# Takeout and square patterns set chunk by chunk in a DFT and squared-ReLU kernel, with a rearranged head and moved folds, on one Trainium2 core

## The chip, the cores and the metric

The kernel runs on one core of one Trainium2 chip. The metric is device time in microseconds (us), measured over several executions of one launch; the profile gives a span of one execution, which is about 2 us shorter here. Engines are named as in the profile: PE is TensorE (matmul), PEld its weight loads, ACT is ScalarE, DVE is VectorE, POOL is GpSimd, SP is SyncE. A run on one core has no second die to be held against, so a run counts as slow here only when it lies more than 1.5% above the fastest of its kernel.

## The reference

```python
def _attn_ref(x):                       # x: (8, 3008, 256)
    X = np.fft.fft(x, axis=1)
    X = np.fft.fft(X, axis=2)
    return X.real.astype(np.float32)

def _moe_ref(x, w_in, w_out):           # x: (24064, 256), w_in: (256, 2048), w_out: (2048, 256)
    h = np.maximum(x @ w_in, 0.0)
    return (h * h @ w_out).astype(np.float32)

def reference(x, moe_w_in, moe_w_out):
    return _moe_ref(_attn_ref(x).reshape(8 * 3008, 256), moe_w_in, moe_w_out)
```

## The kernel before

The kernel folds each batch of `x` by its symmetries (VectorE adds, "fold"), multiplies it by cosine and sine tables (the "DFT", also called stage 1), and folds the feature DFT into the first weight matrix (`G1`, `G2`, `G3`). Outputs come in mirrored pairs: sequence rows k and 3008 - k share the products with `G1` and `G2`. There are 8 x 1505 = 12040 pairs. They are cut into 25 chunks: chunks 0 and 1 of 256 pairs (8 steps each), chunks 2 to 23 of 512 pairs (16 steps each), chunk 24 of 264 pairs. So steps 0 to 15 are chunks 0 and 1, steps 16 to 31 chunk 2, steps 32 to 47 chunk 3, steps 48 to 63 chunk 4. A letter in `KINDS` says how a step makes the two sides of its pairs:

```python
    KINDS = ["rrrrrrrrrrrrrrrr"] * 3 + ["rrrrrrrrdrrrrrrr"] * 3 + ["rrrrrrdrrrdrqrdr"] + ["rrdrqrdrrrdrqrdr"] * 8 + ["rrrrrrrdqrqdrqdr"] + ["qdqrdqrdqrqdrqdr"] * 8 + ["rrdrdrrdrrdrdrrd"]
    SQA = [()] * 6 + [(2, 6)] * 9 + [(1, 4, 6)] * 9 + [()]    # which pairs of steps ScalarE squares
```

A plain step, `r`, takes three matmuls of 512 columns and two ScalarE relus. A takeout, `d` or `q`, takes two matmuls: before the second one, VectorE (`d`), or ScalarE followed by GpSimd (`q`), copies the first product out, and VectorE later makes the mirrored side from that copy.

```python
    def x_front(c, u):                    # r: G1 and G2 products, relu
        # ... matmuls with G1 (start) and G2 into xb ...
        act(r_s(c, u), xb, AF.Relu, scale=-1.0)                              # L606
        return (c, u, xb, None)

    def x_take(c, u):                     # d or q: G1 product alone, taken out to T
        # ... matmul with G1 into xb ...
        X = edge(c, u)                                                       # L633, VectorE
        if KINDS[c][u] == "q":
            act(T, xb, AF.Copy, bias=0.0, scale=-2.0)                        # L649
            nc.gpsimd.tensor_tensor(T, T, X, op=ALU.add)                     # L650
        else:
            stt(out=T, in0=xb, scalar=-2.0, in1=X, op0=ALU.mult, op1=ALU.add)  # L652
        return (c, u, xb.unsqueeze(1), T)

    def x_back(cur):                      # two steps (LAG) later
        if T is not None:
            # ... matmul with G2 into xb ...
            act(r_s(c, u), xb, AF.Relu, scale=-1.0)                          # L662
            # a step later, VectorE: max(xb + T, 0) reversed into the mirrored side, L663
            return
        # ... matmul with G3 into xb ...
        relu_d(c, u, lambda o, i: act(o, xb[:, :, i], AF.Relu, scale=-1.0))  # L670

    def x_square(cur):                    # every second step, over two steps' h
        if u // 2 in SQA[c]:
            # ... two ScalarE squares of half the tile, L679 and L680 ...
            return
        vt(h2, h2, h2, op=ALU.mult)                                          # L682, VectorE
```

`xb` is one of six PSUM tiles, which the DFT also uses. A chunk's output matmuls (`po`) start when its last square has been issued. The program fixes the order of each engine's instructions. The fold of a batch needs that batch of `x`, 3 MB, whose load is issued inside the fold of the batch before, since there is only one buffer `x4`:

```python
    def fold_ops(b):
        # pair, pair0: adds of x rows and mirrored rows from x4 into u        L333, L337
        ops = [f for s in range(2) for f in (pair(s, 0), pair(s, 1), pair0(s))]
        if b + 1 < B:
            ops.append(lambda: load_x(b + 1))     # POOL issues the DMAs once the adds are done
        # ... half, edges, feat: 14 more VectorE operations, L345 to L361 ...
```

`spread` deals operations evenly over a range of steps, and `FOLD` says over which part of a batch's steps a fold is dealt (batch 1 is steps 32 to 79):

```python
    spread(rd1[2:], 1, 8)                 # reduction for the second sine table
    spread(fo, 7, 12)                     # second half of batch 0's fold
    spread(tr1[0:5], 5, 8)                # Sin and Cos of the second table (ScalarE)
    spread(tr1[5:], 8, 9)
    spread(mi1, 9, 12)
    spread(stage1_ops(0, 1, True), 11, 15)   # second DFT of batch 0
    FOLD = {0: [(1, 0.5, 0.66)], 1: [(2, 0.02, 0.28), (3, 0.3, 0.56), (4, 0.58, 0.85)],
            2: [(5, 0.06, 0.96)], 3: [(6, 0.04, 0.96)], 4: [(7, 0.04, 0.85)]}
    ST1 = {0: (0.66, 0.98)}
    # ... in the loop over steps:
        if len(made) > SQ:                # SQ = 3: squares are issued three steps after the relus
            retire()
```

## Time and profile before

| | before |
|---|---|
| time, median of 4 runs | 615.67 us (615.24 to 615.78) |
| span of the profiled run | 613.2 us |
| matmuls, streamed columns | 4631; 1,380,424 |

The page's first part gives busy time, share of the span and instructions of each engine; its fourth part gives the chain of work that ended last, by engine:

```profile
PE 592.0 (97%) x4631; PEld 443.1 (72%) x4631; DVE 493.4 (80%) x855; ACT 522.9 (85%) x949; POOL 146.6 (24%) x138
...
PE 94%; ACT 2%; DMA 2%; DVE 1%; issue 0%; POOL 0%; DVEq 0%; POOLq 0%; ACTq 0%
```

PE bounds the kernel, but 97% does not say how tightly. The Trainium skill, "Perfetto Trace Analysis", Tensor Engine Instruction, says that the end of a matmul is estimated from its size, and "Trainium Kernel Development and Optimization", Performance Expectations, calls matmul busy time a bad metric. The trace agrees: 512-column matmuls are shown 379 ns long, yet start every 216 ns. So PE time is counted here by starts: in PE's instructions in order of time, the spacing of two starts less the columns of the first times 0.4236 ns is called *extra*. Packed matmuls have next to none. Summed up over the trace of before:

| stretch | us |
|---|---|
| until the first matmul starts | 11.0 |
| streaming of all columns but the last matmul's | 584.6 |
| extra, 0 to 20 us | 3.1 |
| extra, 20 to 45 us | 6.7 |
| extra, 45 us to the end | 3.4 |
| last matmul's start to the end | 4.3 |

There are two ways to shorten it: fewer columns, or the 6.7 us of the head. Here PE in order of time in the head (start, us, engine, line, operation, tiles, count, and in brackets the idle time before it and what ended it):

```profile
31.76 0.38 PE L73 MATMUL xb<-qt,G 128*128 128x256 f16 x2 [0.88 <-ACT h L606]
...
33.40 0.38 PE L73 MATMUL xb<-qt,G 128*128 128x256 f16 x2 [0.83 <-ACT h L606]
...
34.72 0.38 PE L73 MATMUL xb<-qt,G 128*128 128x256 f16 x2 [0.50 <-ACT h L606]
...
36.91 0.38 PE L73 MATMUL xb<-qt,G 128*128 128x256 f16 x2 [1.38 <-ACT h L606]
```

In this stretch PE stands before the third product of each step until ScalarE has done the relu. The first output matmul starts at 40.26 us, so PE has nothing else to do.

### The profile page before, as it was taken

What the parts mean: (1) busy time and instruction counts of PE and PEld (TensorE: products, weight loads), DVE (VectorE), ACT (ScalarE), POOL (GpSimd) and SP (SyncE); (2) the same over time, 40 slices, a digit from 0 to 9 for tenths busy, and PEclk for the clock granted to TensorE, in tenths of its full rate; (3) what the DMA queues carried; (4) which work ended last, traced back from release to release, by engine and by line L of the source; (5) the groups of instructions that cost most, each with busy time, mean ns of one, the idle gap of its engine ahead of it and who ended that gap; (6) DMA issues with size and microseconds to landing.
All of it is one profiled execution on the core that took longest, in us unless ns stands there. A gap on an engine that the chain in (4) does not pass through costs nothing.

```text
span 613.2 us, 12145 instructions
## 1 busy us (share of the span) xinstructions
PE 592.0 (97%) x4631; PEld 443.1 (72%) x4631; DVE 493.4 (80%) x855; ACT 522.9 (85%) x949; POOL 146.6 (24%) x138
## 2 busy tenths in 40 slices
PE   2879999999999999999999999999999999999997
PEld 1556677777777777777777778877787778877786
DVE  8789788976578868886888675799998999999870
ACT  5787888777888898888988888999999999999971
POOL 8303023300050002400101010433333334333200
PEclk9999999999999999999999999999999999999999
DMA  8947498673293134832232213332232322332212
GB/s 267 256 91 196 74 237 218 126 190 68 40 247 57 52 43 70 230 61 41 55 60 41 41 51 46 62 42 55 44 58 56 43 56 58 44 60 54 57 52 71
DMA packets 41824, 56.25 MB, mean 92 GB/s; under 512 B 8158, under 2 KB 37138, under 8 KB 41766
## 3 DMA queue, kind: packets, MB, share of 16 engines
q1 hardware_dynamic: 33878, 29.05, 25.2%
q0 software_dynamic: 7840, 26.40, 17.2%
q8 instruction: 36, 0.59, 0.4%
q14 instruction: 22, 0.18, 0.1%
q10 hardware_dynamic: 48, 0.02, 0.0%
HBM read 29.02 MB, written 24.64 MB: 88 GB/s over the span
## 4 chain that ended last, share of the span: by engine, by line
PE 94%; ACT 2%; DMA 2%; DVE 1%; issue 0%; POOL 0%; DVEq 0%; POOLq 0%; ACTq 0%
PE po L73 54%; PE xb L73 34%; PE pf L73 6%; DMA x<-in_x_dram,idx 2%; ACT h L606 1%; DVE u L333 1%; ACT h L670 1%; ACT cosT L260 0%; ACT G L309 0%; ACT G L308 0%; ACT sinT L264 0%; DVE h L682 0%; DVE v L345 0%; DVE tm L236 0%; DVE qt L426 0%
## 5 line engine op out<-in xcount | busy, mean ns | idle before, releaser
L73 PE MATMUL po<-wout,h 128*128 128x256 f16 x3024 | 450.1, 272 | 0.0
L73 PEld LDWEIGHTS <-h 128*128 128x128 f16 x3024 | 286.0, 98 | 112.2
L73 PE MATMUL xb<-qt,G 128*128 128x512 f16 (+16 forms) x824 | 230.9, 321 | 4.5 <-ACT h L606 3.7
L682 DVE TENSOR_TENSOR h<-h 128x2048 f16<-128x2048 f16 (+1 forms) x147 | 176.0, 1201 | 4.6 <-ACT h L670 4.6
L650 POOL TENSOR_TENSOR bs<-bs,h 128x512 f32<-128x512 f32 x68 | 93.5, 1375 | 345.1 <-ACT bs L649 299.8
L606 ACT ACTIVATE h<-xb 128x512 f16<-128x512 f32 (+1 forms) x229 | 139.0, 607 | 28.4 <-PE xb L73 27.7
L670 ACT ACTIVATE h<-xb 128x512 f16<-128x512 f32 (+1 forms) x239 | 139.9, 592 | 26.3 <-PE xb L73 22.1
L73 PEld LDWEIGHTS <-G 128*128 128x128 f16 x1336 | 127.2, 98 | 30.2 <-issue 5.9
L73 PE MATMUL xb<-pt,G 128*128 128x512 f16 (+16 forms) x512 | 146.4, 323 | 0.1
L663 DVE CUSTOM_DVE_ANT_0 h<-xb,bs 128x512 f16<-128x512 f32 (+2 forms) x161 | 104.7, 654 | 43.5 <-ACT h L662 43.5
L662 ACT ACTIVATE h<-xb 128x512 f16<-128x512 f32 (+1 forms) x155 | 96.0, 620 | 8.0 <-PE xb L73 6.5
L652 DVE SCALAR_TENSOR_TENSOR bs<-xb,h 128x512 f32<-128x512 f32 (+1 forms) x87 | 58.2, 669 | 21.0 <-PE xb L73 17.9
L633 DVE TENSOR_SCALAR h<-eb,gE 128x512 f16<-128x512 f16 (+1 forms) x155 | 66.6, 431 | 0.5 <-DMA eb<-qt 0.5
L557 ACT ACTIVATE os<-po 128x512 f32<-128x512 f32 x94 | 58.0, 617 | 9.4 <-PE po L73 8.9
L680 ACT ACTIVATE h<-h 128x1024 f16<-128x1024 f16 x45 | 48.7, 1082 | 0.0
L679 ACT ACTIVATE h<-h 128x1024 f16<-128x1024 f16 x45 | 47.8, 1063 | 0.0
L649 ACT ACTIVATE bs<-xb 128x512 f32<-128x512 f32 x68 | 42.8, 630 | 0.5
L333 DVE TENSOR_TENSOR u<-x 127x765 f16<-127x765 f32 x32 | 29.7, 948 | 1.8 <-DMA x<-in_x_dram 1.6
L101 POOL DMA_INDIRECT x<-in_x_dram,idx x18 | 26.9, 1492 | 5.5 <-issue 4.8
L124 POOL DMA_DIRECT2D x<-in_x_dram x14 | 8.2, 589 | 76.2 <-DVE u L337 75.3
L73 PEld LDWEIGHTS <-w 127*128 127x128 f16 (+1 forms) x192 | 21.6, 118 | 5.7 <-issue 0.7
L351 DVE TENSOR_TENSOR w<-v 127x381 f16<-127x381 f16 x64 | 21.9, 368 | 0.0
(103 smaller groups left out, 217.9 us busy)
## 6 DMA issues: line engine op xcount, KB each, us to landing
out_dram<-os SPq DMA_DIRECT2D x157, 128.0 KB
x<-in_x_dram POOLq DMA_DIRECT2D x14, 756.0 KB, 11.2
wst<-in_moe_w_in_dram POOLq DMA_DIRECT2D x4, 512.0 KB, 7.3
eb<-qt SPq DMA_DIRECT2D x14, 128.0 KB
x<-in_x_dram SPq DMA_DIRECT2D x2, 756.0 KB
wout<-in_moe_w_out_dram POOLq DMA_DIRECT2D x4, 256.0 KB, 10.3
x<-in_x_dram,idx POOLq DMA_INDIRECT x18, 12.4
gE<-G SPq DMA_DIRECT2D x16, 0.2 KB
```

The costliest lines, as they stand in the source:

```text
L73: nc.tensor.matmul(o, l, r, start=start, stop=stop, skip_group_check=True)
L557: act(os_, po, AF.Copy, bias=0.0, scale=HS * HS)
L606: act(r_s(c, u), xb, AF.Relu, scale=-1.0)
L633: ts(out=X, in0=ebc[c][:, 0:n], scalar1=gE2[:, u : u + 1], scalar2=None, op0=ALU.mult)
L650: nc.gpsimd.tensor_tensor(T, T, X, op=ALU.add)
L652: stt(out=T, in0=xb, scalar=-2.0, in1=X, op0=ALU.mult, op1=ALU.add)
L662: act(r_s(c, u), xb, AF.Relu, scale=-1.0)
L663: mirrors.append((DLAG[KINDS[c][u]], lambda: relu_d(c, u, lambda o, i: nc.vector._custom_dve(TENSOR_ADD_SAT, out=o[:, 0, :], in0=xb[:, 0, ...
L670: relu_d(c, u, lambda o, i: act(o, xb[:, :, i], AF.Relu, scale=-1.0))
L679: act(h2[:, 0:nf], h2[:, 0:nf], AF.Square)
L680: rest.append(lambda: act(h2[:, nf:], h2[:, nf:], AF.Square))
L682: vt(h2, h2, h2, op=ALU.mult)
```

## The change

The intent is to take columns off PE where ACT and DVE had room, and to fill PE's holes in the head. Takeouts go from 155 to 200 and ScalarE squares from 45 to 63, each chunk with a pattern of its own. A new kind `v` is a plain step whose mirrored relu is done by VectorE. Operations of the head and folds of batches 1 to 4 move.

```diff
-    KINDS = ["rrrrrrrrrrrrrrrr"] * 3 + ["rrrrrrrrdrrrrrrr"] * 3 + ["rrrrrrdrrrdrqrdr"] + ["rrdrqrdrrrdrqrdr"] * 8 + ["rrrrrrrdqrqdrqdr"] + ["qdqrdqrdqrqdrqdr"] * 8 + ["rrdrdrrdrrdrdrrd"]
-    SQA = [()] * 6 + [(2, 6)] * 9 + [(1, 4, 6)] * 9 + [()]
+    KINDS = ["vrvrrrrrrrrrrrrr"] + ["rrrrrrrrrrrrrrrr"] + ["rvvrrvrrrrrrrrrr"] + ["rrrrrrrrrrrdrrqr"] + ["rdqqrrqrdrrrqrrq"] + ["rrrqrrrrqrqrdddq"] + # ... chunks 6 to 18 ...
+            ["qqdrddrdrqqdrqdq"] + # ... chunks 20 to 24 ...
+    SQA = [()] + [(3,)] + [(2,)] + [(0, 4, 5)] + [(0, 2, 5, 6)] + # ... + [(1, 4, 5, 6, 7)] for chunk 19 ...
...
+        if KINDS[c][u] == "v":
+            relu_d(c, u, lambda o, i: ts(out=o, in0=xb[:, :, i], scalar1=-1.0, scalar2=0.0,
+                                         op0=ALU.mult, op1=ALU.max))
+            return
...
-    spread(rd1[2:], 1, 8)
-    spread(fo, 7, 12)
-    spread(tr1[0:5], 5, 8)
-    spread(tr1[5:], 8, 9)
-    spread(mi1, 9, 12)
-    spread(stage1_ops(0, 1, True), 11, 15)
-    FOLD = {0: [(1, 0.5, 0.66)], 1: [(2, 0.02, 0.28), (3, 0.3, 0.56), (4, 0.58, 0.85)],
+    spread(rd1[2:], 0, 5)
+    spread(fo, 8, 12)
+    spread(tr1[0:5], 8, 11)
+    spread(tr1[5:], 11, 12)
+    spread(mi1, 11, 12)
+    spread(stage1_ops(0, 1, True), 14, 15)
+    FOLD = {0: [(1, 0.504, 0.773)], 1: [(2, 0.02, 0.256), (3, 0.232, 0.697), (4, 0.562, 0.876)],
...
-    ST1 = {0: (0.66, 0.98)}
+    ST1 = {0: (0.845, 0.944)}
...
-        if len(made) > SQ:
+        while len(made) > (1 if made and made[0][0] < 2 else SQ):
             retire()
```

(A new rule for when the edge rows of a chunk are spread is there to make the new patterns legal.)

More of the change, by code (lines that the diff above doesn't have):

```diff
@@ L487 @@
         g += n
-    KINDS = ["rrrrrrrrrrrrrrrr"] * 3 + ["rrrrrrrrdrrrrrrr"] * 3 + ["rrrrrrdrrrdrqrdr"] + ["rrdrqrdrrrdrqrdr"] * 8 + ["rrrrrrrdqrqdrqdr"] + ["qdqrdqrdqrqdrqdr"] * 8 + ["rrdrdrrdrrdrdrrd"]
-    SQA = [()] * 6 + [(2, 6)] * 9 + [(1, 4, 6)] * 9 + [()]
+    KINDS = ["vrvrrrrrrrrrrrrr"] + ["rrrrrrrrrrrrrrrr"] + ["rvvrrvrrrrrrrrrr"] + ["rrrrrrrrrrrdrrqr"] + ["rdqqrrqrdrrrqrrq"] + ["rrrqrrrrqrqrdddq"] + ["rrrrrrqrqqdrqrdd"] + ["rrdrqddrrdrrdrqr"] + ["rqddrrqrrdrdrrqr"] + ["qddrqrdrrrdrddrr"] + ["dqdrdrdrrrdqdrdr"] + ["qrdrrdddrrdrqrqr"] + ["qrdrdrdrrqdrdrdr"] + ["rrqddrqrrrdrddqr"] + ["rrddqdqqrrdqdqdd"] + ["rrrrrrqdqdddrqrd"] + ["ddqrdqrdqqrddqrr"] + ["qddrdqrdqrqdrqqr"] + ["qdqqdqrqqrqdrqrq"] + ["qqdrddrdrqqdrqdq"] + ["qddrdqdrqrqdrqdr"] + ["qdqrdqrqdrqdrqqr"] + ["qrqddqrddrqdrqqr"] + ["qdqqdqvdqrqdrqdr"] + ["rddddddrdrdrdrdd"]
+    SQA = [()] + [(3,)] + [(2,)] + [(0, 4, 5)] + [(0, 2, 5, 6)] + [(0, 4, 6)] + [(2, 3)] + [(4,)] + [(5, 6)] + [(2, 5, 6)] + [(3, 7)] + [(0, 6)] + [(0, 2, 6)] + [(2, 4, 6)] + [(2, 3)] + [(1, 4, 6, 7)] + [(1, 2, 6)] + [(1, 4, 6)] * 2 + [(1, 4, 5, 6, 7)] + [(1, 4, 6)] * 3 + [(1, 4, 6, 7)] + [()]
     gE = const.tile([P, NFC], F16, name="gE")
@@ L738 @@
         side.setdefault(c * (c - 1) // 2, []).extend([lambda c=c: gmat(c), lambda c=c: gneg(c)])
-    spread(rd1[2:], 1, 8)
-    spread(fo, 7, 12)
-    spread(tr1[0:5], 5, 8)
-    spread(tr1[5:], 8, 9)
-    spread(mi1, 9, 12)
-    spread(stage1_ops(0, 1, True), 11, 15)
-    FOLD = {0: [(1, 0.5, 0.66)], 1: [(2, 0.02, 0.28), (3, 0.3, 0.56), (4, 0.58, 0.85)],
+    spread(rd1[2:], 0, 5)
[5 more added lines that the diff above has]
+    FOLD = {0: [(1, 0.504, 0.773)], 1: [(2, 0.02, 0.256), (3, 0.232, 0.697), (4, 0.562, 0.876)],
             2: [(5, 0.06, 0.96)], 3: [(6, 0.04, 0.96)], 4: [(7, 0.04, 0.85)]}
-    ST1 = {0: (0.66, 0.98)}
+    ST1 = {0: (0.845, 0.944)}
     EGRP = {1: [2, 3, 4], 4: [5, 6, 7]}
+    e_done = {}
     for b in range(B - 1):
@@ L759 @@
         spread(stage1_ops(b + 1, 0, b + 1 in INL) + stage1_ops(b + 1, 1, b + 1 in INL), at(lo), at(hi))
+        if b + 1 in INL:
+            e_done[b + 1] = at(hi)
         if b in EGRP:
@@ L762 @@
             side.setdefault(at(0.97), []).append(lambda bb=b + 1: e_row(bb))
+            e_done[b + 1] = at(0.97) + 1
         elif b + 1 not in INL:
@@ L768 @@
     for si, (c, u) in enumerate(steps):
-        if u == 0 and KINDS[c].strip("r"):
-            late = any(chunks[c][3][-1][0] == b + 1 != chunks[c][3][0][0] for b in EGRP)
-            side.setdefault(si - (1 if late else 6), []).append(lambda c=c: e_spread(c))
+        if u == 0 and KINDS[c].strip("rv"):
+            lead = max([si - 6] + [e_done.get(seg[0], 0) for seg in chunks[c][3]])
+            side.setdefault(lead, []).append(lambda c=c: e_spread(c))
     LAG = 2
@@ L793 @@
         take = [mmq.pop(0) for _ in range(-(-len(mmq) // max(1, due - si)))]
-        flight.append((x_front if KINDS[c][u] == "r" else x_take)(c, u))
+        flight.append((x_front if KINDS[c][u] in "rv" else x_take)(c, u))
         h = len(take) // 2
@@ L809 @@
             rest.pop()()
-        if si + 1 < len(steps) and KINDS[steps[si + 1][0]][steps[si + 1][1]] != "r":
+        if si + 1 < len(steps) and KINDS[steps[si + 1][0]][steps[si + 1][1]] not in "rv":
             edge(*steps[si + 1])
-        if len(made) > SQ:
+        while len(made) > (1 if made and made[0][0] < 2 else SQ):
             retire()
```

## The prediction

> **What bounds the kernel now.** TensorE. The page gives PE 97% busy, ACT 85%, DVE 80%, POOL 24% of 613.2 us; the chain that ended last is 94% PE. Ends of matmuls are modelled (the Trainium skill, "Trainium Kernel Development and Optimization", Performance Expectations, calls matmul busy time a bad metric), so I used spacing of starts in the timeline: 256-column matmuls start 108 ns apart, 512-column ones 216 to 217. 1,380,424 streamed columns at about 0.4236 ns make 584.8 us. From 45 us on, starts are packed: some 4 us over pure streaming in 568. The rest is the head: 11 us before the first matmul and about 7 us of gaps at 20 to 38.4 us, where the chain is ScalarE relus 0.48 us apart and PE waits on them (up to 1.4 us each). The windows show ACT 0.85 to 0.91 and DVE 0.64 to 0.82 busy from 150 to 400 us, both 0.93 to 0.97 from 400 to 550, still without PE gaps.
>
> **What the change does.** Takeouts (one 512-column matmul less each) go from 155 to 200, most new ones in chunks 3 to 14; chunks 16 to 23 hardly change. The instruction order gives 21,800 columns less: 9.2 us of PE. Back-to-back spacings in the trace price the rest: ScalarE pass 0.477, a pair of square halves 1.89, DVE square 1.13, edge scaling 0.26, DVE takeout add 0.60, mirrored add 0.60, POOL add 1.375 us.
> - 23 more VectorE takeouts, 22 more ScalarE/GpSimd ones, 6 mirrored relus on DVE, 18 more squares on ScalarE: ACT about +21 us, DVE +33, POOL +30. ACT and DVE approach 90% of the span.
> - Edge scaling averages 641 ns where it overlaps a POOL add, 345 where not; more POOL adds may cost DVE 5 us more.
> - Head: two of chunk 0's relus leave ACT (0.95 us), the second table's Sin/Cos (about 3.2 us of ACT) comes later, and output matmuls start at step 11 instead of 14, filling holes. Adding ACT spacings along the new order, PE passes the ACT-bound stretch some 2 us sooner with more already done: about 3.5 us gained. The second DFT stands as one block before step 15; its last sums may cost back up to 1 us.
>
> **On the critical path.** All 9.2 us, while ACT and DVE keep up; about 3.5 us of the head. ACT and DVE additions are off the path except in overfilled chunks. Per-chunk sums put ACT at or over the PE time in chunks 4, 19 and 23 (ratio 1.0 to 1.04) and DVE in chunk 14 (about 1.05), with runs of six takeouts; POOL adds in chunks 3 to 6 can stand behind the x loads that POOL issues. With six PSUM buffers I expect 1 to 4 us of new PE gaps there.
>
> 613.2 - 9.2 - 3.5 + 2 to 3 gives a span near 603, and a time near 604.5 us (ratio 0.982). Range 600.5 to 609.5. Chances: faster by over 2%: 0.38; within 2%: 0.60; slower: 0.02.
>
> **What would show it.** Matmuls fall from 4631 to 4575. PE gaps between 20 and 40 us shrink from 7 to about 3 us; output matmuls appear near 33 us, not 40. ACT busy rises to about 545, DVE to 530, POOL to 177 us. New PE waits on ACT relus or DVE mirrored adds sit in chunks 4, 14, 19, 23 and total under 4 us.
>
> **What would make it wrong.** If the queues absorb the crowded chunks, 601 to 603. If POOL adds stuck behind loads, or DVE slowed by POOL, hold PSUM buffers, gaps eat most of the 9 us: 608 to 612.

## More of the kernel before

Stretches of the profile of before (start and end; length; then busy us of PE, PEld, DVE, ACT, POOL with counts; granted PE clock; DMA share; GB/s):

```profile
20.00:45.00 25.00, 19.98 (x147) 14.31 (x146) 19.56 (x41) 21.54 (x45) 2.04 (x3) 1.00 0.80 154
75.00:105.00 30.00, 30.00 (x252) 21.56 (x251) 26.63 (x49) 24.68 (x45) 11.14 (x12) 1.00 0.90 220
480.00:510.00 30.00, 30.00 (x224) 21.98 (x223) 28.88 (x46) 27.75 (x50) 11.57 (x8) 1.00 0.34 53
```

The second and third stretch have no PE gap, the second even with DMA at 90%.

DVE in order of time, as the fold of batch 3 begins in the profile of before:

```profile
89.21 1.21 DVE L682 TENSOR_TENSOR h<-h 128x2048 f16<-128x2048 f16 x1
92.03 1.82 DVE L333 TENSOR_TENSOR u<-x 127x765 f16<-127x765 f32 x2 [1.61 <-DMA x<-in_x_dram]
```

DVE waited 1.6 us for the load of batch 3, and nothing came of it.

## The result

| | before | after |
|---|---|---|
| time, median of 4 runs | 615.67 us | 608.86 us (608.63 to 609.20) |
| ratio, 95% interval | | 0.9891 (0.9874 to 0.9908) |
| span of the profiled run | 613.2 us | 606.8 us |

A ratio here is the mean time of one kernel's fast runs over that of the other's of the same rounds, so it is not quite the ratio of the medians. The change is a gain of 1.1%, within the 2% that count as "same"; the predicted 604.5 us was 4.4 us too low, with the measurement inside the range.

The page of the changed kernel (first and fourth part):

```profile
PE 585.2 (96%) x4575; PEld 439.4 (72%) x4575; DVE 527.6 (87%) x961; ACT 534.1 (88%) x951; POOL 174.7 (29%) x160
...
PE 87%; ACT 5%; DMA 3%; POOL 2%; DVE 1%; issue 1%; DVEq 0%; ACTq 0%; POOLq 0%
```

The chain now runs through POOL for 2% of the span (0% before), and DMA has 3% of it in place of 2% and ACT 5% in place of 2%. The same stretches of the changed kernel:

```profile
20.00:45.00 25.00, 23.12 (x179) 17.56 (x177) 23.33 (x46) 22.19 (x46) 2.63 (x3) 1.00 0.86 169
75.00:105.00 30.00, 26.41 (x209) 18.66 (x207) 20.87 (x45) 24.20 (x43) 10.56 (x12) 0.94 0.81 183
480.00:510.00 30.00, 29.45 (x225) 21.82 (x223) 25.96 (x46) 30.00 (x52) 8.83 (x8) 1.00 0.22 45
```

The head has filled up: PE starts 179 matmuls there instead of 147. The second stretch lost 3.6 us of PE time, at a clock of 0.94, with DVE busy 20.9 us of 30 where it had been busy 26.6. In the third, ACT is busy throughout and PE has small gaps. The sum by starts:

| us | before | after | difference |
|---|---|---|---|
| streaming | 584.6 | 575.4 | -9.2 |
| extra, 20 to 45 us (head) | 6.7 | 3.1 | -3.7 |
| extra, 75 to 125 us | 0.6 | 5.9 | +5.3 |
| extra, 480 to 510 us | 0.1 | 1.1 | +1.0 |
| all the rest | 21.1 | 21.3 | +0.2 |
| span | 613.2 | 606.8 | -6.4 |

Both gains came in as predicted, and 6.3 us went elsewhere, 5.3 of them in one place. PE in order of time there, in the changed kernel:

```profile
85.82 0.60 PE L73 MATMUL po<-wout,h 128*128 128x256 f16 x4
90.01 0.38 PE L73 MATMUL xb<-qt,G 128*128 128x481 f16 x2 [3.59 <-DVE bs L652]
90.23 0.60 PE L73 MATMUL po<-wout,h 128*128 128x256 f16 x4
90.67 0.38 PE L73 MATMUL xb<-pt,G 128*128 128x481 f16 x2
90.90 0.92 PE L73 MATMUL po<-wout,h 128*128 128x256 f16 x4
91.61 0.64 PE L73 MATMUL xb<-qt,G 128*128 128x481 f16 x2
92.08 1.02 PE L73 MATMUL po<-wout,h 128*128 128x256 f16 x4
```

PE waits for a takeout on DVE; by starts this gap is 3.75 us. Then the same four output matmuls that took 0.60 us take 0.92 and 1.02: the clock has halved. DVE in order of time says what the takeout waited for:

```profile
80.92 0.62 DVE L351 TENSOR_TENSOR w<-v 127x381 f16<-127x381 f16 x2
88.39 0.96 DVE L333 TENSOR_TENSOR u<-x 127x765 f16<-127x765 f32 x1 [6.86 <-DMA x<-in_x_dram]
89.27 0.69 DVE L652 SCALAR_TENSOR_TENSOR bs<-xb,h 128x512 f32<-128x512 f32 x1
```

The first add of batch 3's fold stood at the head of DVE's queue 6.9 us before its data came, and the takeout stood behind it. (That ACT, DVE and GpSimd are strict FIFO, that is, run their instructions in the order of issue, is what the Trainium skill says in "Perfetto Trace Analysis", Tensor Engine Instruction; for DVE these lines agree, with 6.86 us waited and the takeout 0.9 us after the add.) The chain that ended last, in order of time, gives the source of the wait:

```profile
70.93 0.54 POOL x L124
...
76.53 11.84 DMA x<-in_x_dram
...
88.39 0.04 DVE u L333
```

From the first issue of the load at 70.93 us to the add at 88.39 us it is 17.5 us. In the kernel before, the same load was first issued at 74.83 us and the add ran at 92.03 us, 17.2 us later. The load is no slower. The difference is the placing: by the rule of `spread`, the load of batch 3 is issued at step 35 in both kernels, its first use is dealt to step 46 before (0.3 of the batch's 48 steps) and to step 42 after (0.232). At about 1.4 us a step, the 7 steps from 35 to 42 last some 10 us, and the load takes 17.

The clock, in one-microsecond stretches of the changed kernel:

```profile
90.00:91.00 1.00, 0.99 (x9) 0.73 (x9) 1.00 (x2) 0.58 (x1) 0.00 (x0) 1.00 0.47 163
91.00:92.00 1.00, 1.00 (x7) 0.57 (x4) 1.00 (x2) 0.62 (x2) 0.00 (x0) 0.51 0.00 0
92.00:93.00 1.00, 1.00 (x7) 0.73 (x6) 1.00 (x4) 0.72 (x2) 0.29 (x1) 0.50 0.00 0
93.00:94.00 1.00, 1.00 (x7) 0.43 (x6) 1.00 (x3) 0.83 (x2) 1.00 (x1) 0.50 0.00 0
94.00:95.00 1.00, 1.00 (x9) 0.73 (x8) 1.00 (x2) 0.64 (x2) 0.94 (x2) 0.78 0.00 0
```

The clock (the third number from the end) is 0.5 for about 3.4 us. Work that takes 3.4 us at half the clock would take half of that at full clock, so it costs about 1.7 us. The Trainium skill, "TensorE: Matmul & The Clock Gate", HAM oscillation, gives the rule "no PE-idle gaps >~3.4µs"; the gap of 3.75 us agrees with it. (It is not a safe limit by these traces; see the last section.)

### The profile page after: what moved, and what is told of

Read it like the earlier page. It is cut to its first block, busy times and chain, and to the rows that moved or that the text cites. A ratio compares the mean times of both kernels' runs of the same rounds, so it can differ in the third digit from the quotient of the medians.

```text
span 606.8 us, 12249 instructions
## 1 busy us (share of the span) xinstructions
PE 585.2 (96%) x4575; PEld 439.4 (72%) x4575; DVE 527.6 (87%) x961; ACT 534.1 (88%) x951; POOL 174.7 (29%) x160
## 3 DMA queue, kind: packets, MB, share of 16 engines
q0 software_dynamic: 7840, 26.40, 17.2%
## 4 chain that ended last, share of the span: by engine, by line
PE 87%; ACT 5%; DMA 3%; POOL 2%; DVE 1%; issue 1%; DVEq 0%; ACTq 0%; POOLq 0%
PE po L73 51%; PE xb L73 30%; PE pf L73 6%; DMA x<-in_x_dram 2%; ACT h L606 1%; POOL x L101 1%; DMA wst<-in_moe_w_in_dram 1%; ACT h L674 1%; ACT h L684 0%; ACT h L662 0%; ACT G L308 0%; ACT G L309 0%; ACT h L683 0%; DVE u L333 0%; ACT cosT L260 0%
## 5 line engine op out<-in xcount | busy, mean ns | idle before, releaser
L650 POOL TENSOR_TENSOR bs<-bs,h 128x512 f32<-128x512 f32 x90 | 122.7, 1364 | 342.2 <-ACT bs L649 230.3
L73 PE MATMUL xb<-qt,G 128*128 128x512 f16 (+16 forms) x768 | 214.1, 322 | 5.8 <-DVE bs L652 3.6
L663 DVE CUSTOM_DVE_ANT_0 h<-xb,bs 128x512 f16<-128x512 f32 (+1 forms) x211 | 133.7, 642 | 24.1 <-ACT h L662 22.1
L686 DVE TENSOR_TENSOR h<-h 128x2048 f16<-128x2048 f16 (+1 forms) x129 | 153.6, 1194 | 0.7 <-ACT h L674 0.6
L662 ACT ACTIVATE h<-xb 128x512 f16<-128x512 f32 (+1 forms) x200 | 126.3, 633 | 16.0 <-PE xb L73 14.1
L606 ACT ACTIVATE h<-xb 128x512 f16<-128x512 f32 (+1 forms) x184 | 115.6, 631 | 13.7 <-PE xb L73 13.2
L674 ACT ACTIVATE h<-xb 128x512 f16<-128x512 f32 (+2 forms) x183 | 112.2, 617 | 14.5 <-PE xb L73 12.7
L652 DVE SCALAR_TENSOR_TENSOR bs<-xb,h 128x512 f32<-128x512 f32 (+1 forms) x110 | 72.8, 661 | 17.3 <-PE xb L73 13.0
L633 DVE TENSOR_SCALAR h<-eb,gE 128x512 f16<-128x512 f16 (+1 forms) x200 | 78.0, 395 | 0.4 <-DMA eb<-qt 0.4
L684 ACT ACTIVATE h<-h 128x1024 f16<-128x1024 f16 x63 | 69.5, 1103 | 0.0
L683 ACT ACTIVATE h<-h 128x1024 f16<-128x1024 f16 x63 | 68.4, 1086 | 0.0
L649 ACT ACTIVATE bs<-xb 128x512 f32<-128x512 f32 x90 | 58.7, 652 | 2.7 <-PE xb L73 1.5
```

The costliest lines, as they stand in the source:

```text
L73: nc.tensor.matmul(o, l, r, start=start, stop=stop, skip_group_check=True)
L633: ts(out=X, in0=ebc[c][:, 0:n], scalar1=gE2[:, u : u + 1], scalar2=None, op0=ALU.mult)
L663: mirrors.append((DLAG[KINDS[c][u]], lambda: relu_d(c, u, lambda o, i: nc.vector._custom_dve(TENSOR_ADD_SAT, out=o[:, 0, :], in0=xb[:, 0, ...
L683: act(h2[:, 0:nf], h2[:, 0:nf], AF.Square)
L684: rest.append(lambda: act(h2[:, nf:], h2[:, nf:], AF.Square))
```

## Experiments

Each kernel ran three rounds against the kernel before on the same chip; the medians of before were 615.42 us (e1 to e4), 614.96 (e5 to e8) and 615.12 (e9 to e12), with single runs from 614.3 to 617.0. Single runs of one kernel also spread over 0.7 to 3.4 us (8.7 with one outlier in e3), so differences under a microsecond are read from the traces, by the same sum of extra time. All results were correct.

| run | median us | ratio (95% interval) | extra 20 to 45 | 75 to 125 | 480 to 510 us | span |
|---|---|---|---|---|---|---|
| before | 615.67 | | 6.73 | 0.64 | 0.09 | 613.2 |
| after | 608.86 | 0.9891 (0.9874 to 0.9908) | 3.07 | 5.92 | 1.13 | 606.8 |
| e1 later folds | 605.08 | 0.9835 (0.9810 to 0.9860) | 3.07 | 2.19 | 1.13 | 602.7 |
| e2 d to q | 608.44 | 0.9879 (0.9852 to 0.9905) | 3.07 | 5.36 | 1.13 | 607.1 |
| e3 filler | 607.17 | 0.9904 (0.9830 to 0.9977) | 3.06 | 2.51 | 1.12 | 605.1 |
| e4 squares of chunk 19 | 609.51 | 0.9902 (0.9879 to 0.9924) | 3.07 | 7.24 | 0.15 | 607.1 |
| e5 patterns alone | 609.15 | 0.9900 (0.9880 to 0.9921) | 6.72 | 2.47 | 1.13 | 606.9 |
| e6 head and folds alone | 614.35 | 0.9981 (0.9949 to 1.0013) | 3.06 | 2.71 | 0.09 | 612.0 |
| e7 e1 and e4 | 603.78 | 0.9818 (0.9794 to 0.9841) | 3.07 | 1.85 | 0.17 | 601.7 |
| e8 e7, squares moved | 606.66 | 0.9852 (0.9824 to 0.9881) | 3.07 | 4.81 | 0.16 | 604.7 |
| e9 after, again | 608.66 | 0.9886 (0.9861 to 0.9912) | 3.07 | 5.71 | 1.13 | 606.7 |
| e10 e7, two takeouts less | 603.30 | 0.9816 (0.9793 to 0.9839) | 3.06 | 0.56 | 0.18 | 601.2 |
| e11 e10, takeouts moved | 604.01 | 0.9816 (0.9800 to 0.9833) | 3.06 | 0.53 | 1.35 | 602.7 |
| e12 e7, late squares in head | 605.57 | 0.9841 (0.9825 to 0.9857) | 4.80 | 2.39 | 0.16 | 604.4 |

The theory: DVE is blocked on the load of batch 3, and that is what takes back 5.3 us. The first rival: chunks 3 to 5 are simply too full of takeouts and GpSimd adds, wherever the fold stands. A second question is why PE could not make it up.

### e1: the folds later

```diff
-1: [(2, 0.02, 0.256), (3, 0.232, 0.697), (4, 0.562, 0.876)]
+1: [(2, 0.02, 0.256), (3, 0.345, 0.60), (4, 0.69, 0.90)]
```

> Only the placing of the folds of batches 3 and 4 is changed in the changed kernel: batch 3's first add moves from step 42 to step 48, batch 4's from 58 to 64. Theory (DVE blocked in order on the x load of batch 3, with a takeout that PE needs queued behind it): the DVE wait on the x DMA falls from 6.9 us to under 1, the PE gap of 3.8 us at 86 us and the half clock after it go away, time 608.9 - 3.75 - 1.65 = about 603.5 us. Rival (chunks 3 to 5 are simply overfilled by takeouts and GpSimd adds): gaps of a similar sum stay somewhere between 75 and 120 us, time above 606.5.

Measured: 605.08 us. Its stretch from 75 to 105 us, to be held against that of the changed kernel above:

```profile
75.00:105.00 30.00, 28.66 (x236) 20.77 (x234) 23.92 (x50) 28.02 (x49) 11.89 (x13) 1.00 0.69 160
```

DVE's wait for `x` in this place is gone, PE's clock stays at 1.00, and the extra time of 75 to 125 us falls from 5.92 to 2.19 us. So the placing of the fold of batch 3 was most of the loss. (The edit moves the fold of batch 4 too, but its first step is 58 in the changed kernel, after the gap at 86 us.) But a gap of 1.5 us remains at 100.7 us, in which PE waits for a mirrored add on DVE: the rival has a part in it.

### e2: the blocked takeout goes to ScalarE and GpSimd

```diff
-["rrrrrrrrrrrdrrqr"]      # chunk 3
+["rrrrrrrrrrrqrrqr"]
```

> One letter changed in the changed kernel: the takeout of step 43 goes to ScalarE with GpSimd instead of VectorE; the fold stays early. Theory that the takeout behind the blocked add makes the wait into a PE gap: the DVE wait for x stays at 6 to 7 us, PE's gap shrinks from 3.8 us to under 1, no half clock, time about 603.5 to 605. Rival (any 7 us of DVE standing still starves PE, through squares and PSUM buffers): gap stays over 2 us, time above 607.

Measured: 608.44 us, within noise of the unmodified change and above the 603.5 to 605 expected. Waits of e2 between 75 and 107 us (who waited for whom: us in total, times, longest):

```profile
DVE u L333 <- DMA x<-in_x_dram: 7.0, 1, 7.0
...
PE xb L73 <- DVE h L663: 2.8, 2, 2.1
...
PE xb L73 <- DVE pt L433: 1.6, 1, 1.6
```

This falls to the rival. The gap at 86 us is gone and the clock stays at 1.00, yet the same 7 us on DVE come back as three smaller gaps, at 91, 102 and 105 us, 4.84 us together. So which instruction stands behind the blocked add decided where PE stopped and whether the clock dropped, but hardly how much was lost (5.36 us extra in place of 5.92): DVE has no room there to make up 7 us. My theory that the single takeout behind it was the cause is wrong.

### e3: useless matmuls ahead of the gap

```diff
+        if si == 44:
+            filler = psx.tile([P, 512], F32, name="filler", tag="x")
+            for _ in range(12):
+                mm(filler, ez[:, 0, 0, :], ez[:, 0, 0:4, :], True, True)
```

> Twelve matmuls of 512 columns with no use (2.6 us of TensorE) are put just ahead of the gap at 86 us, nothing else changed. Theory that about 1.65 of the 5.4 us lost there is the TensorE clock halved after the idle gap: the gap shrinks to about 1.2 us, the clock stays at 1.00 between 90 and 95 us, and the kernel with more work is faster: about 607.2 us. If the half clock does not come from the idleness, the time stays at 608.9; if the gap is not waited out at a fixed time, it rises to 611.5.

Measured: a median of 607.17 us with 2.6 us more work for TensorE (one of the four runs took 615.25, which makes the ratio wide). DVE's wait was 7.4 us, half a microsecond longer than in the profile of after, and still the span is 1.7 us shorter. Two stretches of e3:

```profile
85.00:90.00 5.00, 3.47 (x21) 1.71 (x19) 1.78 (x4) 1.08 (x2) 0.00 (x0) 1.00 0.84 155
90.00:95.00 5.00, 5.00 (x45) 3.76 (x44) 5.00 (x8) 4.62 (x8) 2.23 (x2) 1.00 0.00 0
```

The clock between 90 and 95 us is 1.00, where it was 0.66 on average in after, and 45 matmuls run there instead of 31. So the half clock does come from the idle gap. What it is worth is the estimate of 1.7 us from the clock record; e3 agrees in sign and rough size only. Of the 1.7 us of span, 0.7 came before 20 us, which the edit does not touch; between 75 and 125 us the extra time fell by 3.4 us for 2.6 us more streaming, a gain of 0.8 us, although DVE's data came half a microsecond later.

### e4: three ScalarE squares in chunk 19 instead of five

```diff
-[(1, 4, 6)] * 2 + [(1, 4, 5, 6, 7)]
+[(1, 4, 6)] * 3
```

> Chunk 19 of the changed kernel gets three ScalarE squares instead of five. Theory (ScalarE overfilled in chunk 19): the three small PE gaps at 492 to 500 us, 1.0 us in sum, go away, time about 607.9. If DVE then takes over as limit, gaps of the same size stay and the time is 608.5 to 609.

Measured: 609.51 us, which misses what was expected, but the trace shows why. The gaps at 492 to 500 us are gone (1.13 to 0.15 us). In the same run DVE waited 7.4 us for `x`, the gap at 86 us was 4.33 us and the extra time there 7.24 instead of 5.92 us. DVE's wait for this load varies by about half a microsecond and more from run to run (6.7 to 7.4 us in after, e2, e3, e4 and e9), and the clock dropped earlier and for longer (0.86 on average from 85 to 90 us, 0.50 from 90 to 95). So chunk 19 was overfilled for ScalarE, 1.0 us worth; the time shows it only once the other loss is away (e7).

### e5 and e6: each half of the change alone

e5 takes the patterns from chunk 3 on and leaves head, folds and squares of chunks 0 to 2 as before; e6 takes all the rest and leaves the old patterns from chunk 3 on.

```diff
# e5, against the changed kernel
-["vrvrrrrrrrrrrrrr"] + ["rrrrrrrrrrrrrrrr"] + ["rvvrrvrrrrrrrrrr"] ; SQA [()] + [(3,)] + [(2,)]
+["rrrrrrrrrrrrrrrr"] * 3                                            ; SQA [()] * 3
 # chunk 23: v to r; spread, FOLD, ST1 and the rule of retire as before
# e6, against the changed kernel
 # KINDS of chunks 0 to 2 kept
-["rrrrrrrrrrrdrrqr"] + # ... the new patterns
+["rrrrrrrrdrrrrrrr"] * 3 + ["rrrrrrdrrrdrqrdr"] + # ... the old ones, and the old SQA from chunk 3 on
```

> The new takeout and square patterns from chunk 3 on, with the head, the folds and the DFT placing of the kernel before. Theory: 9.2 us of columns gained, no head gain, 1.0 us lost in chunk 19, and with batch 3's fold at its old step the DVE wait for x stays near 1.6 us, yet DVE is so full in chunks 3 to 5 that 1 to 3 us of PE gaps come up between 80 and 110 us: time 615.5 - 9.2 + 1.0 + 2 = about 609 us (607.5 to 610). Rival (patterns cost nothing where the fold is not early): about 607.

> The changed kernel with the old takeout and square patterns from chunk 3 on, so the new head and the early folds alone. Head theory: 4.0 us gained between 15 and 45 us. The early fold of batch 3 stays, so DVE waits about 7 us for x; with few takeouts and DVE otherwise light in chunks 3 to 5 the lost time is made up later: PE gaps of 0 to 1.5 us between 80 and 110 us, time 611.5 to 613. Rival (a wait of 7 us on DVE costs PE about 5 us whatever the load): about 616.

Measured: e5 609.15 us, the time that the theory had: 9.2 us of columns gained, 1.0 lost in chunk 19, and PE gaps of 0.45 us at 106 and 1.38 us at 121 us, the second later than the 80 to 110 us expected. In both gaps PE waits for a mirrored add, and DVE waited for no DMA between 75 and 125 us (its 0.4 us for `x` in this run is at 11 us), so here it is DVE's work alone. e6: 614.35 us, above the 613 expected, with an interval that holds 1. Its waits between 75 and 105 us:

```profile
DVE u L333 <- DMA x<-in_x_dram: 5.8, 1, 5.8
...
PE xb L73 <- DVE h L663: 2.0, 1, 2.0
```

The head gain is there in full (3.06 us extra, as in after), and the early fold costs 2.1 us (2.71 less 0.64) at the old, lighter patterns. So neither expectation held exactly: a wait of 5.8 us on DVE costs 2.1 us where DVE has room, and one of 6.9 us costs 5.3 where it has none. The patterns alone cost 1.8 us (2.47 less 0.64) between 75 and 125 us. The two together cost more than 2.1 + 1.8 = 3.9 us. The 1.7 us of the clock could account for the excess (5.6 against 5.3 measured), but that is not shown: e2 lost 4.7 us (5.36 less 0.64) at full clock.

### e7 and e8: both repairs, and an attempt to fill DVE's idle time

e7 is e1 and e4 together. e8 adds this:

```diff
-[(0, 4, 5)] + [(0, 2, 5, 6)]      # ScalarE squares of chunks 3 and 4
+[(0,)] + [(0, 1, 2, 5, 6)]
```

> Later folds (as the first experiment) and chunk 19 with three ScalarE squares (as the fourth) together. Both losses are at different times and should add: 605.1 - 1.0 = about 604.1 us, gaps of the 100 us region about 1.7 us, none at 490 us.

> As the run before, and two of chunk 3's squares go from ScalarE to DVE, where DVE stands idle at 82 to 90 us, one of chunk 4's from DVE to ScalarE. Theory that the gap left at 100 us is DVE's backlog after it stood idle: the gap falls from 1.5 us to under 0.5, time about 602.7 us. If ScalarE is the limit there instead, the gap stays or grows: 604 or more.

Measured: e7 603.78 us, as expected; the two losses add. e8 606.66 us, a miss. Stretches from 90 to 105 us of e7, then e8:

```profile
90.00:105.00 15.00, 13.84 (x105) 10.02 (x104) 14.97 (x28) 14.28 (x26) 8.43 (x9) 1.00 0.40 105
```

```profile
90.00:105.00 15.00, 11.34 (x84) 8.02 (x83) 13.86 (x20) 10.26 (x19) 8.24 (x8) 1.00 0.43 111
```

What came out is the number that went with ScalarE as the limit, but the trace doesn't show that: ACT is busy 10.3 of 15 us in e8. One of the moved squares ran in DVE's idle time at 87.8 us, the other stood at 91.4 us ahead of the fold, whose first add came at 92.5 instead of 90.2 us; PE waited 2.6 us for the DFT's sums on DVE and 1.3 us for a mirrored add. Here one more square of 1.2 us on DVE in front of a full stretch went with 3.0 us more extra time (4.81 against 1.85), more than its own length. That points to DVE as the limit there, and asks for the opposite experiment.

### e9 to e11: less for DVE at 90 to 100 us

e9 is the changed kernel again, as the base on this chip. e10 is e7 with two takeouts of chunk 4 made plain; e11 also moves takeouts of chunk 3.

```diff
 # e10, against e7 (chunk 4)
-["rdqqrrqrdrrrqrrq"]
+["rdrrrrqrdrrrqrrq"]
 # e11, against e10 (chunk 3)
-["rrrrrrrrrrrdrrqr"]
+["rrrrrrrrrdrdrdrr"]
```

> The changed kernel itself once more, as the base of the runs of this chip: 608.6 to 609.7 us, with the wait of DVE for x at 6.5 to 7.5 us.

> Later folds and three squares in chunk 19 (the seventh run), and two ScalarE/GpSimd takeouts of chunk 4 (steps 50 and 51) made plain: DVE loses 1.7 us of work at 92 to 100 us, ScalarE none, TensorE gets 0.43 us more. Theory (DVE's backlog makes the gap at 100 us): the gap of 1.3 to 1.5 us falls under 0.4, time 603.8 - 1.1 + 0.43 = about 603.1. Rival (ScalarE, also full there, makes it): gap stays, 604.2.

> As the run before, with three VectorE takeouts instead of two takeouts in chunk 3 (steps 41, 43, 45), into the time in which DVE stands idle: TensorE 0.22 us less than the run before, time about 602.9; if DVE's backlog grows again, a gap over 0.5 us at 100 us and 603.5 or more.

Measured: e9 608.66 us, with DVE's wait 6.7 us. e10 603.30 us; its stretch from 90 to 105 us:

```profile
90.00:105.00 15.00, 15.00 (x113) 10.72 (x111) 13.92 (x26) 14.89 (x27) 7.67 (x7) 1.00 0.71 180
```

The gap is gone (0.56 us extra, as in before), with ACT fuller than in e7 and DVE emptier. ScalarE was not the limit. (The edit also takes two GpSimd adds away; whether DVE's own work or its waits for those adds mattered was not told apart.) It paid 0.43 us of columns for it, so against e7 the span gained 0.5 us. e10 has the lowest median here (e7 is not told apart from it by the ratios), 1.8% faster than the kernel before and 0.9% than the change; its interval reaches over 2%, so whether it passes that mark stays open.

e11 took 604.01 us, above the 602.9 expected. It kept the gap at 100 us closed, but got a new one of 1.2 us at 480 us, some 380 us after anything that its edit touches. Its trace shows there a DVE square of 2.18 us in place of 1.22, started 0.19 us after a POOL add. The last section follows this up; that it caused e11's gap is likely from the trace (PE waited 1.06 us for a mirrored add that stood behind it), and was not tried.

### e12: squares of the head late again

```diff
-        while len(made) > (1 if made and made[0][0] < 2 else SQ):
+        if len(made) > SQ:
```

(against e7)

> The seventh run's kernel with the squares of chunks 0 and 1 retired as late as in the kernel before, so that output matmuls start at step 14 instead of 11. Theory that the early output matmuls fill PE's holes in the head: gaps between 15 and 45 us rise from 4.2 to about 6 us and the time by about 2 us, to 605.8. If the freed relus and moved table alone made the head gain, the time stays at 603.8.

Measured: 605.57 us. Output matmuls start at 35.99 instead of 32.7 us, and the extra time of the head rises from 3.07 to 4.80 us. So early squares give 1.7 of the head's 3.7 us. The other 2 us are left for the freed relus and the moved operations by subtraction; none of these was tried alone.

## Why the prediction was right or wrong

**PE is the limit, and 9.2 us of columns: right.** The trace shows 4575 matmuls, 21,800 columns less, and 9.2 us less streaming.

**3.5 us of the head: right.** It was 3.7 us, and e6 shows it without the new patterns. Output matmuls were predicted near 33 us and started at 32.7. The up to 1 us that the DFT block was allowed to cost is not seen in that sum.

**Busy times: right for DVE and POOL, high for ACT.** DVE 527.6 (530 said), POOL 174.7 (177), ACT 534.1 (545). The estimate summed back-to-back spacings and left out that the tails of relus, shown as busy, vanish where an idle ACT fills up (a 128x512 relu is shown 615 ns long in before, and back to back they start about every 478 ns); that this is the 11 us is likely and was not followed up.

**New PE gaps of 1 to 4 us in chunks 4, 14, 19 and 23: the step that failed.** The sum was 613.2 - 9.2 - 3.5 + 2 to 3; the last term measured 6.3. Only chunk 19 did what was said, 1.0 us (e4 closed it). Between 125 and 480 us, which holds chunk 14, nothing was lost (2.03 against 1.90 us), and chunk 23 shows no gap either: queues absorbed those. The other 5.3 us lie at the end of chunk 3 and the start of chunk 4. They come from the fold of batch 3 moved four steps forward, ahead of a load that takes 17 us (e1), and from DVE too full to make up the wait (e2, e6, e10). About 1.7 us of them are the halved clock, by the clock record (e3 shows that the gap causes it). With the fold moved back, a gap of 1.3 to 1.5 us does stand in chunk 4 (e1, e7), of the size predicted, but it is DVE's and not ScalarE's (e10).

The prediction looked at the moved folds only in the head. It did name loads as a danger, but in the wrong place: GpSimd adds behind the issue of loads, where it was a VectorE add in front of the landing of one. (The first GpSimd add of the changed kernel ran at 92.7 us, after the gap.) That the time came within the stated range, 0.6 us under its upper end, is therefore in part luck: the prediction gave 608 to 612 us to another cause. The profile before held the warning: DVE waited 1.6 us for this very load with the fold four steps later. A step there lasts about 1.4 us; four steps earlier makes that about 7 us, an estimate that needed no experiment.

What stays open: whether the gap at 100 us of e1 and e7 comes from DVE's work alone or also from the edge rows' DMAs behind the load (DVE waited 2.2 us for one in e7 from 87.7 us). e10 still has that wait, 2.2 us up to 90.6 us, and no gap, so the wait alone does not make it; a run without the wait and with all of DVE's work was not made.

## What to carry to other kernels

When a change moves the first use of a buffer that a DMA fills, count the time from the issue of the load to that use, against the load's measured time, and look for existing waits on it, even ones that cost nothing yet. An engine with slack forgave most of a wait of several microseconds here (2.1 us lost of 5.8), and a change that filled that engine at the same time took that forgiveness away (5.3 us lost of 6.9). A PE gap of 3.75 us cost about half as much again through the clock, while gaps of 2.3 and 2.8 us left the clock alone (e2, e8); so a long gap can cost more than its length.

## What the Trainium skill lacked or had wrong

- "GPSIMD Engine Reference", Key points, says that GpSimd shares its SBUF interfaces with VectorE and that there is contention, without a number. (That whichever starts first holds the shared pair for the whole instruction, and the other blocks, is not lacking: it stands in "SBUF — State Buffer", SBUF: two separate sides.) The runs add these sizes. Of the 128x512 edge scalings on DVE that started well inside a POOL add (more than 0.05 us after its start and 0.2 us before its end), all 374 in thirteen traces (e9, the same kernel as after, left out) ended 0.15 us after the add did (0.77 us on average in place of 0.34). Of the DVE squares that started so, 35 of 43 ended 1.08 us after it (up to 2.18 us in place of 1.22); the other eight did not wait, and the POOL add under way was then shown 2.5 to 4.6 us long in place of 1.36, so the order of the shown starts does not always tell who goes first. Where the POOL add started second, DVE was not slowed (squares 1217 ns with and 1216 without).
- "TensorE: Matmul & The Clock Gate", HAM oscillation: the limit of about 3.4 us agrees as far as gaps inside the kernel go. Gaps of 3.6, 3.75 and 4.3 us (e9, after, e4) halved the clock for 3.4, 3.4 and 6.8 us, gaps of 2.3 and 2.8 us (e2 and e8) did not. But when the clock drops varies: with a gap from 86.3 to 90.0 us it halved at 91.0 us, after a microsecond of full work; in e4 it halved at 88.6 us, 2.5 us into its gap; and after the last matmul's start it halved 2.3 (e8) to 5.6 us (e3) later. The drops in e4 and at the end of e8 came before 3.4 us of idleness, which the rule does not say, so a gap under 3.4 us is not shown to be safe.
